# Weight tiles fetched with a shift of three bytes, decoded in three VectorE passes, and the range guard run in the loop on a second read

## The chip, the cores and the metric

The kernel runs on one core of one Trainium2 chip. The metric is the device time of one execution in microseconds (us); 598.0 us is the median of three runs before the change. The engines named below are PE (TensorE, matmuls), PEld (its weight loads), DVE (VectorE), ACT (ScalarE), POOL (GpSimd) and SP (SyncE, which here issues nearly all transfers).

## The reference

An attention-like recurrence over 768 steps (batch 4, 8 heads of 48) feeds a gated feed-forward layer:

```python
for t in range(S):
    cur = np.einsum('bhd,bhe->bhde', u[None] * kt, vt)
    y[:, :, t] = np.einsum('bhd,bhde->bhe', rt, state + cur)
    state = wt[:, :, :, None] * state + np.einsum('bhd,bhe->bhde', kt, vt)
...
gate = 1.0 / (1.0 + np.exp(-(x @ w_gate)))
val = x @ w_val
return (gate * val @ w_out).astype(np.float32)
```

Here x holds the 3072 rows of y with 384 columns; w_gate and w_val are 384 x 1536, w_out is 1536 x 384. The three weight matrices come as 64-bit floats, and the kernel turns them into 32-bit floats itself, by moving bits.

## The kernel before

**Stages.** The 768 steps are cut into 6 chunks of 128; chunk n of batch element b is one attention stage q = 4 n + b, so there are 24 stages. Each stage loads `pin` (decays, k and r, heads on the partitions) and `tok` (r, k and v, time on the partitions), runs two scans on VectorE (prep_k, prep_r), small matmuls on PE (turn_k, scores, sums, mix), a guard on ScalarE (`guard`, a Square with an accumulator) and ends by writing the 384 columns of x for its 128 rows, split into a high part (float32r) and the rest. The feed-forward layer takes 512 rows at a time (n = 0 to 5) and goes through 12 tiles of d_ff (f = 0 to 11). For each f: 9 matmuls into `pg` (gate), 9 into `pu` (value), a sigmoid on ScalarE, the product on VectorE (hidden), its high and low part (hidden_hi on ScalarE, hidden_lo on VectorE), and 9 matmuls into `po` (down). `pg` and `pu` have one buffer each.

**Weights.** A weight tile f is 128 partitions by 1152 words of 64 bits (the gate's, the value's and the output's 384 columns). `fetch` loads it into `raws[f]`, 9216 bytes a partition. `word(f, i)` is the view of its low (i = 0) or high (i = 1) 32-bit words, at a stride of two words. VectorE puts the 32-bit float together in `full` (one buffer): w_body shifts the high word by 3 and masks it (L271), w_sign takes over the top two bits (L275), w_tail the low word's top three (L279). w_hi rounds it to float32r on ScalarE (L284), w_lo takes the rest on VectorE (L287). Both parts are laid over the raw tile. Beside that `w_guard` squares the high words as 32-bit floats on ScalarE and runs a Relu over the squares, each with an accumulator (L265, L266); the two sums per tile tell later whether any weight is outside the range that the decoding takes.

**Head and loop.** The first 13 stages, the decoding of all 12 weight tiles and the feed-forward layer of n = 0 and 1 (in groups of 256 rows, for which `up` and `down` take two stages at a time) stand in an order that a planner (`Plan`) makes when the kernel is built: a list schedule by engine with a cost for each step, ranks for the attention stages and weight tiles (TURNS), a fixed order of transfers (COMES), and counts of free buffers (ROOM). From n = 2 on the order is written out: one step is one f, three steps (i = 0, 1, 2) carry one attention stage of the next chunk. `steps(q)` cuts that stage into `trio[i][0..2]`. In a step every engine takes its part in this order: gate, sigmoid, trio[i][0], value, hidden, hidden_hi, hidden_lo, trio[i][1], the down matmuls of the step before, trio[i][2]. Of this, at i = 0: turn_k and take_k (ScalarE copies kT, L377), then scores_sums, in which `pairs` (L390) is followed by `add_up` (L437), which reads kT. At i = 1: state_mix, take_y, turn_x, take_x, and the loads for stage q + 2. At i = 2: bonus3, bonus4, prep_r of stage q + 1 and, as the last of them, guard of stage q + 1 on ScalarE (L368). Engines run their own instructions in order and wait for each other by semaphores; SP issues its transfers in order.

**The end.** In the first step of n = 5 `check_bounds` compares all accumulators with their limits, adds the results up through a matmul and writes `flag`. If it is set, a general version (`general`) runs after the loop.

Of the kernel before, what the change touches and what calls it, by code (L numbers as in the profile page):

```python
# [9 lines left out]
F32 = mybir.dt.float32  # L10
F32R = mybir.dt.float32r
BF16 = mybir.dt.bfloat16
I32 = mybir.dt.int32
I64 = mybir.dt.int64
AF = mybir.ActivationFunctionType
ALU = mybir.AluOpType
AX = mybir.AxisListType
# [3 lines left out]
DM, DFF = 384, 1536  # L21
P = 128
C = 128
NC_ = S // C
NG = B * NC_
# [3 lines left out]
WW = 520  # L29
NFF = DFF // P  # L30
NKT = DM // P
TINY = 2.0 ** -14
LEAST = float.fromhex("0x1.2p-15")
TURNS = "c0 w0 c1 w1 c2 w2 w3 w4 w5 c3 w6 w7 w8 c4 w9 w10 w11 c5 c6 c7 c8 c9 c10 c11 c12"
COMES = "p0 t0 ub w0 p1 p2 t1 w1 w2 p3 t2 t3 w3 w4 w5 t4 p4 w6 w7 w8 w9 w10 w11 p5 t5 t6 p6 t7 p7 p8 t8 t9 p9 p10 p11 t10 t11 p12 p13 t12 t13"
# [9 lines left out]
def general(ctx: ExitStack, tc: tile.TileContext, dec, tok, wts, u, out, whi, wlo, ident):  # L45
# [72 lines left out]
    def feed(n, b, turned):  # L118
# [6 lines left out]
        for f in range(NFF):  # L125
            for s, acc in enumerate((pg, pu)):
                for k in range(NKT):
                    cols = slice(s * DM + k * P, s * DM + (k + 1) * P)
                    for j, (w, a) in enumerate(((wlo, xhi), (whi, xlo), (whi, xhi))):
                        nc.tensor.matmul(acc[:, :C], lhsT=w[f][:, cols], rhs=a[:, k], start=k == 0 and j == 0, stop=k == NKT - 1 and j == 2)  # L130
            nc.scalar.activation(gate, pg[:, :C], AF.Sigmoid)
            nc.vector.tensor_tensor(out=h, in0=pu[:, :C], in1=gate, op=ALU.mult)
# [72 lines left out]
def tile_kernel(ctx: ExitStack, tc: tile.TileContext, dec: bass.AP, tok: bass.AP, wts: bass.AP, u: bass.AP, out: bass.AP):  # L205
    nc = tc.nc
    const = ctx.enter_context(tc.tile_pool(name="const", bufs=1))
    own = ctx.enter_context(ExitStack())
    own.enter_context(tc.manual_schedule())
    p1 = own.enter_context(tc.tile_pool(name="p1", bufs=1))  # L210
# [25 lines left out]
    for s in range(2):  # L236
        part = after[s * HC:(s + 1) * HC]
        nc.gpsimd.affine_select(
            out=part, in_=part, pattern=[[1, HC]], compare_op=ALU.is_gt, fill=0.0, base=0, channel_multiplier=-1,
# [1 line left out]
    ub = const.tile([P, DM], F32, name="ub")  # L241
    acc_d = const.tile([L, NG], F32, name="acc_d")
    acc_x = const.tile([P, NG], F32, name="acc_x")
    acc_s = const.tile([P, NFF], F32, name="acc_s")
    acc_t = const.tile([P, NFF], F32, name="acc_t")
    fine = const.tile([P, 4, NG], F32, name="fine")
    nc.gpsimd.memset(fine, 1.0)
    flag = const.tile([1, 1], I32, name="flag")
    ones = const.tile([P, 1], F32, name="ones")
# [4 lines left out]
    raws, fulls, whi, wlo = {}, {}, [None] * NFF, [None] * NFF  # L254

    def fetch(f):
        raws[f] = const.tile([P, 3 * DM], I64, tag=f"w{f}", name=f"wraw{f}")
        nc.sync.dma_start(raws[f], wts[f])

    def word(f, i, dtype=I32):  # L260
        return raws[f].bitcast(dtype).rearrange("a (c w) -> a c w", w=2)[:, :, i]

    def w_guard(f):
        sq = p1.tile([P, 3 * DM], BF16, tag="sq", name=f"sq{f}")
        nc.scalar.activation(sq, word(f, 1, F32), AF.Square, accum_out=acc_s[:, f:f + 1])  # L265
        nc.scalar.activation(sq, sq, AF.Relu, bias=1.0, scale=-1.0 / TINY ** 2, accum_out=acc_t[:, f:f + 1])  # L266

    def w_body(f):
        t = p1.tile([P, 3 * DM], I32, tag="full", name=f"full{f}")
        fulls[f] = t  # L270
        nc.vector.tensor_scalar(out=t, in0=word(f, 1), scalar1=3, scalar2=0x3FFFFFF8, op0=ALU.logical_shift_left, op1=ALU.bitwise_and)  # L271

    def w_sign(f):
        t = fulls[f]
        nc.vector.scalar_tensor_tensor(out=t, in0=word(f, 1), scalar=-0x40000000, in1=t, op0=ALU.bitwise_and, op1=ALU.bitwise_or)  # L275

    def w_tail(f):
        t = fulls[f]
        nc.vector.scalar_tensor_tensor(out=t, in0=word(f, 0), scalar=29, in1=t, op0=ALU.logical_shift_right, op1=ALU.bitwise_or)  # L279

    def w_hi(f):
        w = const.tile([P, 2, 3 * DM], F32R, tag=f"w{f}", name=f"w{f}")
# [82 lines left out]
    def guard(q):  # L365
        junk = p1.tile([L, 2, 516], BF16, tag="junk", name=f"junk{q}")
        both = eg[q][:, 1:1 + 2 * 519].rearrange("a (i c) -> a i c", c=519)[:, :, :516]
        nc.scalar.activation(junk, both, AF.Square, accum_out=acc_d[:, q:q + 1])  # L368

# [105 lines left out]
    def parts_x(q):  # L475
        if q // B not in x:
            x[q // B] = p2.tile([P, 2, NKT, B * C], F32R, tag="x", name=f"x{q // B}")
        return (x[q // B][:, j, :, q % B * C:(q % B + 1) * C] for j in range(2))

    def take_x(q):  # L480
        hi, _ = parts_x(q)
        nc.scalar.activation(hi, bank["x", q], AF.Copy, accum_out=acc_x[:, q:q + 1])

# [16 lines left out]
    def gate(n, f, i0, i1):  # L500
        hid["g", n, f, i0] = up(0, "pg", n, f, i0, i1)

    def sigmoid(n, f, i0, i1):
        sg = hid["s", n, f, i0] = stage.tile([P, (i1 - i0) * C], F32, tag="sg", name=f"sg{n}_{i0}_{f}")
        nc.scalar.activation(sg, hid["g", n, f, i0], AF.Sigmoid)  # L505

# [51 lines left out]
    def check_bounds():  # L558
        nc.vector.tensor_scalar(out=fine[:L, 0], in0=acc_d, scalar1=2.0 ** 90, scalar2=None, op0=ALU.is_le)
        nc.vector.tensor_scalar(out=fine[:, 1], in0=acc_x, scalar1=0.0, scalar2=0.0, op0=ALU.mult, op1=ALU.is_equal)  # L560
        nc.vector.tensor_scalar(out=fine[:, 2, :NFF], in0=acc_s, scalar1=1e10, scalar2=None, op0=ALU.is_le)
        nc.vector.tensor_scalar(out=fine[:, 3, :NFF], in0=acc_t, scalar1=0.0, scalar2=None, op0=ALU.is_equal)
        count = p1.tile([P, 1], F32, name="count")
        nc.vector.tensor_reduce(out=count, in_=fine, op=ALU.add, axis=AX.XY)
        total = att_bank("total")
        nc.tensor.matmul(total[:1, :1], lhsT=ones, rhs=count, start=True, stop=True)
        nc.vector.tensor_scalar(out=flag, in0=total[:1, :1], scalar1=float(P * 4 * NG), scalar2=None, op0=ALU.not_equal)


    plan = Plan(ROOM)  # L570
# [3 lines left out]
    def add(name, engine, cost, after, rank, f=None, *args, take=(), give=()):  # L574
        plan.add(name, engine, cost, after, rank, f and (lambda: f(*args)), take, give)

    add("ub", "SP", 0.6, [], comes["ub"], lambda: nc.sync.dma_start(ub, u.partition_broadcast(P)))
    for q in range(3 * B + 2):
        k = rank.get(f"c{q}", 99)
# [33 lines left out]
    for f in range(NFF):  # L613
        k = rank[f"w{f}"]
        add(f"words{f}", "SP", 4.2, [], comes[f"w{f}"], fetch, f)
        add(f"wg{f}", "ACT", 2.8, [f"words{f}", f and f"wg{f - 1}"], k, w_guard, f)
        add(f"wb{f}", "DVE", 0.76, [f"words{f}", f and f"wb{f - 1}"], k, w_body, f, take=["full"])
        add(f"ws{f}", "DVE", 1.36, [f"wb{f}"], k, w_sign, f)
        add(f"wt{f}", "DVE", 1.36, [f"ws{f}"], k, w_tail, f)
        add(f"wh{f}", "ACT", 1.15, [f"wt{f}", f"wg{f}"], k, w_hi, f)  # L620
        add(f"wl{f}", "DVE", 1.3, [f"wh{f}"], k, w_lo, f, give=["full"])
    for g, (n, i0, i1) in enumerate(GROUPS):
        m = i1 - i0
        for f in range(NFF):
            a, name = (n, f, i0, i1), f"{g}_{f}"
            k = 100 + f + LAGS[g]
# [45 lines left out]
    for n in range(2, NC_):  # L672
        for j in range(B):
            trio = steps((n + 1) * B + j) if n + 1 < NC_ else nothing
            for i in range(3):
                a = (n, 3 * j + i, 0, B)
                if a != ahead:
                    gate(*a)
                sigmoid(*a)
                trio[i][0]()  # L680
                value(*a)
                hidden(*a)
                hidden_hi(*a)
                hidden_lo(*a)
                trio[i][1]()
                if last:
                    down_turned(*last.pop())
                trio[i][2]()
                last.append(a)
                if n == NC_ - 1 and j == 0 and i == 0:  # L690
                    check_bounds()
# [37 lines left out]
```

## Time and profile before

| What | us |
|---|---|
| runs shown | 595.76, 598.0, 598.21 |
| median | 598.0 |
| span of the profiled execution, first to last instruction | 593.7 |
| around the span, by the median | 4.3 |
| PE busy, of the span | 555.1 |
| VectorE busy | 332.6 |
| ScalarE busy | 200.2 |

No time is listed for the profiled execution but its span; the runs lie 2.1 to 4.5 us above it. Rows of the profile start with the engine or the line: `L275 DVE ...` is line 275 on VectorE, `out<-in` names the tiles, `x12` counts the instructions, then come busy time and mean length in ns, then the idle time of that engine just ahead of them and who ended it. Rows of a timeline start with two times, start and length.

### The profile page before, as it was taken

To read this page: it belongs to the slowest core of one execution; us is meant where nothing else is said; L and a number is where in the kernel's file an instruction comes from. 1 tells how busy PE (TensorE), PEld (TensorE's weight loads), DVE (VectorE), ACT (ScalarE), POOL (GpSimd) and SP (SyncE) were. 2 spreads that over 40 slices of the span, in tenths; PEclk is the share of its full clock that TensorE was granted. 3 is DMA by queue.
4 is the path that set the end of the run, shared out by engine and by line. 5 is a ranking of instruction groups with operands and counts; after the bars stand their busy time and mean duration, and the time that the engine had idled before them with its cause. 6 is when DMAs were issued, how large, how long until landed. Compare 5 with 4: busy or idle time off the path is not lost.

```text
span 593.7 us, 14287 instructions
## 1 busy us (share of the span) xinstructions
PE 555.1 (93%) x6330; PEld 478.6 (81%) x6330; DVE 332.6 (56%) x571; ACT 200.2 (34%) x397; POOL 96.4 (16%) x86
## 2 busy tenths in 40 slices
PE   4477799999999999999999999999999999999995
PEld 3366699999999999888888888888888888788884
DVE  4989889989675762254644644644544554212121
ACT  2648783434333322322212322212322212222221
POOL 3342011102220503002202202202202200000000
PEclk9998799999999999999999999999999999999999
DMA  8887930022243221122032042032032000100001
GB/s 238 269 332 285 363 94 2 1 88 71 73 135 97 82 70 60 54 87 73 18 88 78 17 135 87 3 87 83 24 124 86 3 1 2 40 15 0 1 0 60
DMA packets 11479, 50.84 MB, mean 86 GB/s; under 512 B 1312, under 2 KB 2464, under 8 KB 9872
## 3 DMA queue, kind: packets, MB, share of 16 engines
q1 hardware_dynamic: 8672, 45.38, 23.7%
q10 hardware_dynamic: 2736, 4.46, 2.0%
q8 instruction: 52, 0.85, 0.6%
q14 instruction: 19, 0.16, 0.1%
HBM read 45.11 MB, written 4.72 MB: 84 GB/s over the span
## 4 chain that ended last, share of the span: by engine, by line
PE 86%; DVE 7%; DMA 3%; issue 1%; ACT 1%; SPq 0%; ACTq 0%; DVEq 0%
PE pu L494 25%; PE pg L494 25%; PE po L546 16%; PE po L529 8%; PE pa L461 3%; PE pa L390 2%; PE pa L400 2%; DMA wraw<-wts 2%; PE pk L373 1%; PE px L473 1%; PE pv L437 1%; DVE eg L341 1%; DMA pin<-dec 1%; PE pa L437 1%; DVE full L275 1%
## 5 line engine op out<-in xcount | busy, mean ns | idle before, releaser
L494 PE MATMUL pu<-x,w 128*128 128x256 f32 (+1 forms) x864 | 171.4, 343 | 0.0
L494 PE MATMUL pg<-x,w 128*128 128x256 f32 (+1 forms) x864 | 169.0, 341 | 1.2 <-DVE w L287 1.2
L494 PEld LDWEIGHTS pg<-x,w 128*128 128x128 f32 x864 | 137.9, 192 | 19.4 <-DVE w L287 1.6
L494 PEld LDWEIGHTS pu<-x,w 128*128 128x128 f32 x864 | 136.7, 192 | 17.1
L512 DVE TENSOR_TENSOR sg<-pu,sg 128x256 f32<-128x256 f32 (+1 forms) x96 | 53.4, 556 | 145.0 <-PE pu L494 144.0
L516 ACT CAST hh<-sg 128x256 fp32r<-128x256 f32 (+1 forms) x96 | 49.1, 512 | 171.2 <-DVE sg L512 170.8
L505 ACT ACTIVATE sg<-pg 128x256 f32<-128x256 f32 (+1 forms) x96 | 46.9, 489 | 139.0 <-PE pg L494 137.7
L546 PE MATMUL po<-hh,w 128*128 128x512 f32 x288 | 89.1, 390 | 0.0
L334 POOL TENSOR_TENSOR bon<-tok,a 128x384 f32<-128x384 f32 x24 | 34.9, 1456 | 277.3 <-DVE a L330 277.3
L520 DVE TENSOR_TENSOR hl<-sg,hh 128x256 fp32r<-128x256 f32 (+1 forms) x96 | 55.2, 575 | 39.1 <-ACT hh L516 39.0
L546 PEld LDWEIGHTS po<-hh,w 128*128 128x128 f32 x288 | 54.1, 188 | 10.8
L546 PE MATMUL po<-hl,w 128*128 128x512 f32 x144 | 58.7, 407 | 0.2 <-DVE hl L520 0.2
L323 POOL TENSOR_TENSOR bon<-tok,ub 128x384 f32<-128x384 f32 x24 | 32.3, 1345 | 114.1 <-DMA tok<-tok 38.4
L529 PE MATMUL po<-w,hh 128*128 128x384 f32 x192 | 49.7, 340 | 0.0
L468 DVE TENSOR_TENSOR bon<-pa,bon 128x192 f32<-128x192 f32 x48 | 15.6, 352 | 48.0 <-PE pa L461 47.9
L529 PE MATMUL po<-w,hl 128*128 128x384 f32 x96 | 34.5, 359 | 6.0 <-DVE hl L520 6.0
L368 ACT ACTIVATE junk<-eg 112x1032 bf16<-112x1032 f32 x24 | 25.6, 1066 | 29.7 <-DVE eg L358 29.6
L529 PEld LDWEIGHTS po<-w,hh 128*128 128x128 f32 x192 | 35.5, 192 | 0.0
L341 DVE TENSOR_TENSOR_SCAN eg<-pin,ends 112x516 f32<-112x516 f32 x24 | 30.0, 1249 | 5.0 <-DMA pin<-dec 5.0
L546 PEld LDWEIGHTS po<-hl,w 128*128 128x128 f32 x144 | 27.0, 188 | 6.2 <-DVE hl L520 0.6
L358 DVE TENSOR_TENSOR_SCAN eg<-pin,heads 112x516 f32<-112x516 f32 x24 | 29.7, 1237 | 0.0
L326 POOL TENSOR_TENSOR bon<-bon,tok 128x384 f32<-128x384 f32 x24 | 27.4, 1140 | 1.7
(68 smaller groups left out, 502.4 us busy)
## 6 DMA issues: line engine op xcount, KB each, us to landing
pin<-dec SPq DMA_DIRECT2D x23, 675.5 KB, 5.3
tok<-tok SPq DMA_DIRECT2D x24, 576.0 KB, 5.8
wraw<-wts SPq DMA_DIRECT2D x12, 1152.0 KB, 12.3
y<-o ACTq DMA_DIRECT2D x11, 256.0 KB, 2.1
y<-o ACTq DMA_DIRECT2D x8, 192.0 KB, 1.9
pin<-dec SPq DMA_DIRECT2D x1, 448.0 KB, 4.0
y<-o SPq DMA_DIRECT2D x1, 256.0 KB, 2.9
pin<-dec SPq DMA_DIRECT2D x1, 227.5 KB, 2.8
```

The source lines that it names most:

```text
L323: nc.gpsimd.tensor_tensor(out=bon[q], in0=tk[q][:, 0:DM], in1=ub, op=ALU.mult)
L326: nc.gpsimd.tensor_tensor(out=bon[q], in0=bon[q], in1=tk[q][:, DM:2 * DM], op=ALU.mult)
L334: nc.gpsimd.tensor_tensor(out=by_head(bon[q]), in0=by_head(tk[q][:, 2 * DM:]), in1=a0, op=ALU.mult)
L341: nc.vector.tensor_tensor_scan(out=e[:, 516:0:-1], data0=t[:, 516:0:-1], data1=ends[:, 516:0:-1], initial=0.0, op0=ALU.mult, op1=ALU.add,)
L358: nc.vector.tensor_tensor_scan(out=e[:, WW:WW + 516], data0=t[:, 0:516], data1=heads[:, 0:516], initial=0.0, op0=ALU.mult, op1=ALU.add,)
L494: nc.tensor.matmul(t, lhsT=w[f][:, cols], rhs=x[n][:, a, k, i0 * C:i1 * C], start=k == 0 and j == 0, stop=k == NKT - 1 and j == 2)
L505: nc.scalar.activation(sg, hid["g", n, f, i0], AF.Sigmoid)
L512: nc.vector.tensor_tensor(out=sg, in0=hid["u", n, f, i0], in1=sg, op=ALU.mult)
L516: nc.scalar.copy(hh, hid["s", n, f, i0])
L520: nc.vector.tensor_tensor(out=hl, in0=hid["s", n, f, i0], in1=hid["hi", n, f, i0].bitcast(F32), op=ALU.subtract)
L529: nc.tensor.matmul(po[n, i][:, :DM], lhsT=h[:, c], rhs=w[f][:, 2 * DM:], start=f == 0 and j == 0, stop=f == NFF - 1 and j == 2,)
L546: nc.tensor.matmul(po[n, k], lhsT=w[f][:, cols], rhs=h, start=f == 0 and j == 0, stop=f == NFF - 1 and j == 2)
```

## The change

The fetch starts 3 bytes into each row, so that byte 3 of a 64-bit word lands at byte 0. The low 32-bit word then holds bits 24 to 55 of the float, and byte 4 holds its top byte. ScalarE's w_top takes that byte, computes 1.125 x + 0.4375, and writes it as an integer over the high word; the lowest five bits of the result are the top five bits of the 32-bit float. VectorE's w_body shifts the low word right by 5, w_join puts the five bits on top. w_sign and w_tail are gone, w_lo stays.

The guard no longer runs over the fetched tiles. In the loop, `see` loads half a weight tile again (576 of 1152 words, unshifted, 576 KB) into the buffer `full`, and one step later `w_guard` runs on it: a Square and two Relus on ScalarE, for values that are too small and too large. 24 halves take the steps from n = 2, f = 0 to n = 4, f = 0. check_bounds compares one more accumulator. The planner's entries change with it.

```diff
     def fetch(f):
         raws[f] = const.tile([P, 3 * DM], I64, tag=f"w{f}", name=f"wraw{f}")
-        nc.sync.dma_start(raws[f], wts[f])
+        nc.sync.dma_start(raws[f].bitcast(U8)[:, :24 * DM - 3], wts[f].bitcast(U8)[:, 3:])
...
-    def w_guard(f):
-        sq = p1.tile([P, 3 * DM], BF16, tag="sq", name=f"sq{f}")
-        nc.scalar.activation(sq, word(f, 1, F32), AF.Square, accum_out=acc_s[:, f:f + 1])
-        nc.scalar.activation(sq, sq, AF.Relu, bias=1.0, scale=-1.0 / TINY ** 2, accum_out=acc_t[:, f:f + 1])
+    def w_top(f):
+        top = raws[f].bitcast(U8).rearrange("a (c w) -> a c w", w=8)[:, :, 4]
+        nc.scalar.activation(word(f, 1), top, AF.Copy, bias=0.4375, scale=1.125)
 
     def w_body(f):
         t = p1.tile([P, 3 * DM], I32, tag="full", name=f"full{f}")
         fulls[f] = t
-        nc.vector.tensor_scalar(out=t, in0=word(f, 1), scalar1=3, scalar2=0x3FFFFFF8, op0=ALU.logical_shift_left, op1=ALU.bitwise_and)
-
-    def w_sign(f):
+        nc.vector.tensor_scalar(out=t, in0=word(f, 0), scalar1=5, scalar2=None, op0=ALU.logical_shift_right)
+
+    def w_join(f):
         t = fulls[f]
-        nc.vector.scalar_tensor_tensor(out=t, in0=word(f, 1), scalar=-0x40000000, in1=t, op0=ALU.bitwise_and, op1=ALU.bitwise_or)
-
-    def w_tail(f):
-        t = fulls[f]
-        nc.vector.scalar_tensor_tensor(out=t, in0=word(f, 0), scalar=29, in1=t, op0=ALU.logical_shift_right, op1=ALU.bitwise_or)
+        nc.vector.scalar_tensor_tensor(out=t, in0=word(f, 1), scalar=27, in1=t, op0=ALU.logical_shift_left, op1=ALU.bitwise_or)
+
+    seen = {}
+
+    def see(g):
+        f, part = divmod(g, PARTS)
+        seen[g] = p1.tile([P, PW], I64, tag="full", name=f"seen{g}")
+        nc.sync.dma_start(seen[g], wts[f][:, part * PW:(part + 1) * PW])
+
+    def w_guard(g):
+        size = seen.pop(g).bitcast(F32).rearrange("a (c w) -> a c w", w=2)[:, :, 1]
+        sq = p1.tile([P, PW], BF16, tag="sq", name=f"sq{g}")
+        few = p1.tile([P, PW], BF16, tag="few", name=f"few{g}")
+        nc.scalar.activation(sq, size, AF.Square, accum_out=acc_s[:, g:g + 1])
+        nc.scalar.activation(few, sq, AF.Relu, bias=1.0, scale=-1.0 / SMALL ** 2, accum_out=acc_t[:, g:g + 1])
+        nc.scalar.activation(few, sq, AF.Relu, bias=-1.0, scale=1.0 / LARGE, accum_out=acc_u[:, g:g + 1])
...
-        nc.vector.tensor_scalar(out=fine[:, 3, :NFF], in0=acc_t, scalar1=0.0, scalar2=None, op0=ALU.is_equal)
+        for i, acc in enumerate((acc_t, acc_u)):
+            nc.vector.tensor_scalar(out=fine[:, 3 + i, :NP_W], in0=acc, scalar1=0.0, scalar2=None, op0=ALU.is_equal)
...
-        add(f"wg{f}", "ACT", 2.8, [f"words{f}", f and f"wg{f - 1}"], k, w_guard, f)
+        add(f"wg{f}", "ACT", 1.15, [f"words{f}"], k, w_top, f)
         add(f"wb{f}", "DVE", 0.76, [f"words{f}", f and f"wb{f - 1}"], k, w_body, f, take=["full"])
-        add(f"ws{f}", "DVE", 1.36, [f"wb{f}"], k, w_sign, f)
-        add(f"wt{f}", "DVE", 1.36, [f"ws{f}"], k, w_tail, f)
-        add(f"wh{f}", "ACT", 1.15, [f"wt{f}", f"wg{f}"], k, w_hi, f)
+        add(f"wt{f}", "DVE", 1.36, [f"wb{f}", f"wg{f}"], k, w_join, f)
+        add(f"wh{f}", "ACT", 1.15, [f"wt{f}"], k, w_hi, f)
...
                 trio[i][1]()
+                guarded = (n - 2) * NFF + 3 * j + i
+                if guarded < NP_W + 1:
+                    if guarded:
+                        w_guard(guarded - 1)
+                    if guarded < NP_W:
+                        see(guarded)
                 if last:
                     down_turned(*last.pop())
                 trio[i][2]()
```

More of the change, by code (lines that the diff above doesn't have):

```diff
@@ L14 @@
 I64 = mybir.dt.int64
+U8 = mybir.dt.uint8
 AF = mybir.ActivationFunctionType
@@ L31 @@
 NKT = DM // P
-TINY = 2.0 ** -14
+SMALL = 2.0 ** -12
+LARGE = 32.0
+PARTS = 2
+NP_W = NFF * PARTS
+PW = 3 * DM // PARTS
 LEAST = float.fromhex("0x1.2p-15")
@@ L243, in tile_kernel @@
     acc_x = const.tile([P, NG], F32, name="acc_x")
-    acc_s = const.tile([P, NFF], F32, name="acc_s")
-    acc_t = const.tile([P, NFF], F32, name="acc_t")
-    fine = const.tile([P, 4, NG], F32, name="fine")
+    acc_s, acc_t, acc_u = (const.tile([P, NP_W], F32, name=n) for n in ("acc_s", "acc_t", "acc_u"))
+    fine = const.tile([P, 5, NG], F32, name="fine")
     nc.gpsimd.memset(fine, 1.0)
@@ L560, in check_bounds @@
         nc.vector.tensor_scalar(out=fine[:, 1], in0=acc_x, scalar1=0.0, scalar2=0.0, op0=ALU.mult, op1=ALU.is_equal)
-        nc.vector.tensor_scalar(out=fine[:, 2, :NFF], in0=acc_s, scalar1=1e10, scalar2=None, op0=ALU.is_le)
-        nc.vector.tensor_scalar(out=fine[:, 3, :NFF], in0=acc_t, scalar1=0.0, scalar2=None, op0=ALU.is_equal)
+        nc.vector.tensor_scalar(out=fine[:, 2, :NP_W], in0=acc_s, scalar1=1e10, scalar2=None, op0=ALU.is_le)
+        for i, acc in enumerate((acc_t, acc_u)):
+            nc.vector.tensor_scalar(out=fine[:, 3 + i, :NP_W], in0=acc, scalar1=0.0, scalar2=None, op0=ALU.is_equal)
         count = p1.tile([P, 1], F32, name="count")
@@ L566, in check_bounds @@
         nc.tensor.matmul(total[:1, :1], lhsT=ones, rhs=count, start=True, stop=True)
-        nc.vector.tensor_scalar(out=flag, in0=total[:1, :1], scalar1=float(P * 4 * NG), scalar2=None, op0=ALU.not_equal)
+        nc.vector.tensor_scalar(out=flag, in0=total[:1, :1], scalar1=float(P * 5 * NG), scalar2=None, op0=ALU.not_equal)
     plan = Plan(ROOM)
```

## The prediction

> **What bounds the kernel now.** I read the page's shares first, then busy time by stage, then the chain of waits in the first 100 us.
>
> ```profile
> span 593.7 us, 14287 instructions
> PE 555.1 (93%) x6330; PEld 478.6 (81%) x6330; DVE 332.6 (56%) x571; ACT 200.2 (34%) x397; POOL 96.4 (16%) x86
> ```
> ```profile
> 0.00:20.00 20.00, 7.13 (x151) 5.71 (x151) 11.00 (x16) 7.43 (x12) 5.36 (x17) 1.00 0.88 238
> 20.00:40.00 20.00, 12.01 (x200) 10.37 (x201) 17.83 (x25) 12.16 (x21) 10.95 (x8) 1.00 0.89 341
> 40.00:60.00 20.00, 15.92 (x260) 14.34 (x259) 18.42 (x28) 14.70 (x26) 4.16 (x4) 0.88 0.72 268
> 60.00:80.00 20.00, 15.90 (x245) 14.33 (x242) 16.81 (x25) 15.85 (x31) 3.86 (x3) 0.87 0.72 261
> 80.00:100.00 20.00, 19.36 (x239) 18.68 (x232) 18.61 (x28) 11.21 (x23) 2.70 (x2) 1.00 0.23 66
> 300.00:400.00 100.00, 100.00 (x1063) 81.41 (x1050) 51.65 (x92) 26.51 (x52) 16.51 (x12) 1.00 0.24 74
> ```
> The columns of a window are its length, then the busy time of PE, PEld, DVE, ACT and POOL, then the granted clock, the DMA share and GB/s. There are two kernels in one span. In the first 80 us PE idles 29 of 80 us (20 minus 7.13, 12.01, 15.92 and 15.90, added up) while VectorE works 18 of each 20. From about 90 us on PE is full: 100.00 of 100 in the loop. So time can be won only in the head, and anything that makes PE wait in the loop is lost whole, however idle ScalarE is there on average (26.51 of 100).
>
> ```profile
> 2.66 11.41 DMA wraw<-wts
> 15.12 1.26 DVE full L275
> 27.30 1.29 DVE full L275
> 41.90 1.27 DVE full L275
> 53.81 1.28 DVE full L275
> 61.30 2.29 PE pg L494 x9
> 70.32 1.32 PE po L529 x6
> ```
> These are pieces of the chain that ended last (start, length, what). The sign pass of L275, which the change deletes, is on it four times. From 70.32 the chain is nearly all PE.
>
> **The change in the head.** It deletes w_sign (L275), the guard's Square and Relu (L265, L266) with their two accumulator reads, and puts one ScalarE Copy per weight tile in their place.
>
> ```profile
> L271 DVE TENSOR_SCALAR full<-wraw 128x1152 int32<-128x1152 int32 x12 | 9.4, 782 | 1.3 <-DMA wraw<-wts 1.3
> L275 DVE SCALAR_TENSOR_TENSOR full<-wraw,full 128x1152 int32<-128x1152 int32 x12 | 16.2, 1350 | 0.0
> L279 DVE SCALAR_TENSOR_TENSOR full<-wraw,full 128x1152 int32<-128x1152 int32 x12 | 17.1, 1426 | 0.0
> ```
> VectorE: 12 x 1.350 = 16.2 us go. The new w_body has one operator where L271 had two; shape and stride are the same, so I take L271's 0.78 us; its ends are 0.78 and 1.35 (L275). w_join has the operands of L279: 1.43, no change. ScalarE's timeline around the second and third tile's guard:
>
> ```profile
> 24.92 1.24 ACT L265 ACTIVATE sq<-wraw 128x1152 bf16<-128x1152 f32 x1
> 26.28 1.16 ACT L266 ACTIVATE sq<-sq 128x1152 bf16<-128x1152 bf16 x1
> 27.62 1.25 ACT L265 ACTIVATE sq<-wraw 128x1152 bf16<-128x1152 f32 x1
> 29.00 1.16 ACT L266 ACTIVATE sq<-sq 128x1152 bf16<-128x1152 bf16 x1
> 30.22 1.15 ACT L284 CAST w<-full 128x1152 fp32r<-128x1152 f32 x1
> ```
> One guard takes 27.62 - 24.92 = 2.70 us of ScalarE, and that goes. w_top reads bytes at a stride of 8 and writes words at that stride. No row has this; the nearest are the cast of L284 (1.15) and the strided Square of L265 (1.25); I take 1.25. So 1.45 us of ScalarE per tile are freed, 17.4 in all.
>
> What of the 16.2 us counts? The chain carries four sign passes ahead of 70.32: 1.26 + 1.29 + 1.27 + 1.28 = 5.1. The fifth tile's is covered: PE's 61.30 group was on the chain then. Later ones run beside a full PE. Off this goes a new wait: w_join needs w_top. For the first tile, landed at 14.07 (2.66 + 11.41), w_top ends about 15.35, and the sign pass of before was due at 15.12: 0.25 us. For later tiles w_top needs only the fetch and can run ahead. If it does not, up to 0.5 us (1.25 minus 0.78) is exposed for each of five tiles, 2.4 in all. **Head: minus 4.9**; ends minus 2.5 and minus 10.6 (rival 2).
>
> The fetch moves 9213 bytes per row from 3 bytes past the row's start, one run as before. I take no cost; no row shows an odd start, so rival 4 prices it. The Trainium skill, page "DMA: Bandwidth & Descriptors", section "How a descriptor splits into AXI transactions", has reads go out from the 256-byte boundary below the start; rows of 9216 bytes would then take 36 transactions either way, and no run here shows it yet.
>
> **The change in the loop.** 24 steps (all of n = 2 and 3, shifted by one) get a half-tile guard on ScalarE: a Square and two Relus of 576 columns, each with an accumulator read. It is issued after trio[i][1], so at i = 2 it stands behind guard(q+1) and ahead of the next step's sigmoid and take_k. Two views of the same step, ScalarE's and PE's timeline (start, length, engine, line, in brackets the idle time before):
>
> ```profile
> 290.65 1.07 ACT L368 ACTIVATE junk<-eg 112x1032 bf16<-112x1032 f32 x1 [2.36 <-DVE eg L358]
> 291.71 0.58 ACT L505 ACTIVATE sg<-pg 128x512 f32<-128x512 f32 x1
> 292.19 0.52 ACT L377 COPY kT<-pk 128x448 f32<-128x448 f32 x1
> 294.23 0.62 ACT L516 CAST hh<-sg 128x512 fp32r<-128x512 f32 x1 [1.52 <-DVE sg L512]
> 298.86 0.60 ACT L505 ACTIVATE sg<-pg 128x512 f32<-128x512 f32 x1 [4.01 <-PE pg L494]
> ```
> ```profile
> 291.07 2.33 PE L494 MATMUL pu<-x,w 128*128 128x512 f32 x9
> 293.33 0.69 PE L390 MATMUL pa<-pin 48*64 48x64 f32 x32
> 293.84 0.62 PE L437 MATMUL pa<-tok,kT 64*64 64x48 f32 x32
> ```
> ScalarE waits for VectorE's scan until 290.65, runs the old guard, then sigmoid and kT with no gap. kT is done at 292.71; PE reads it at 293.84 (L437, add_up). So 1.13 us of room, and the new guard goes in right there.
>
> Its length follows from the old guard's start-to-start times at 1152 columns, above, and one shorter cast:
>
> ```profile
> 41.94 0.41 ACT L516 CAST hh<-sg 128x256 fp32r<-128x256 f32 x1 [2.06 <-DVE sg L512]
> ```
> Square to Relu 1.36, Relu to the next user of its buffer 1.34, Relu to another operation 1.22: together 3.92. Casts took 0.41 at 256 columns and 0.62 at 512, so 0.82 ns a column, 0.47 us for the 576 columns each pass lacks: 3.92 - 1.41 = 2.5 us. The sigmoid then starts at 294.21, kT ends 1.00 later (0.48 and 0.52) at 295.21, and add_up is late by 295.21 - 293.84 = 1.37 us. PE has nothing else in its order to do.
>
> There are 8 such places: i = 2 of four j in n = 2 and four in n = 3, each followed by a step with take_k. **8 x 1.37 = plus 11.0**. Where the passes wait for no buffer, 0.12 (1.34 - 1.22) goes twice: 2.26 us of guard and 9.0 in all; with 0.1 more than my value it is 11.8. At i = 0 and i = 1 the guard fits: after the cast at 294.23, even 1.4 later, ScalarE has until the sigmoid of 298.86, which shifts by the same 1.4.
>
> The rereads go on SP's queue: each waits for the Square before it, and the later pin and tok loads stand behind it.
>
> ```profile
> tok<-tok SPq DMA_DIRECT2D x24, 576.0 KB, 5.8
> ```
> A tok load has the reread's 576 KB and lands 5.8 us after its issue. The tightest reread is issued at about 292.5 and lands by 298.3; its guard then ends near 300.8, under a microsecond after the delayed sigmoid is due and more than a microsecond before VectorE needs it. The loads behind it are for stage q + 2 while q is worked on, so they have all of stage q + 1 to land in, and some microseconds on SP cost nothing; without that cover the guard's wait would be passed on to PE, up to 5.8 at each place. check_bounds gets one more VectorE operation on an already waiting PE: plus 0.2, from this row and the larger sum after it.
>
> ```profile
> L562 DVE TENSOR_SCALAR fine<-acc_t 128x12 f32<-128x12 f32 x1 | 0.2, 164 | 0.0
> ```
> **Sum:** -4.9 + 11.0 + 0.2 = +6.3. On the span that is 600.0. The median of the runs shown, 598.0, lies 4.3 over this span, which I keep as it is: **604.3 us**.
>
> **The rivals.**
> 1. *The loop hides the guard* (faster). For it: ScalarE is 26.51 busy of 100 there. Against: the room ahead of L437 is 1.13 us and the guard fills 2.5. It decides at 1.13: under that, or with guard(q+1) 1.4 us earlier, nothing stalls, and -4.9 + 0.2 gives 593.3.
> 2. *The head gives more* (no change). VectorE ran seven sign passes before PE was full, the first and the last of them:
> ```profile
> 15.04 1.35 DVE L275 SCALAR_TENSOR_TENSOR full<-wraw,full 128x1152 int32<-128x1152 int32 x1
> 83.42 1.35 DVE L275 SCALAR_TENSOR_TENSOR full<-wraw,full 128x1152 int32<-128x1152 int32 x1
> 45.02 0.41 DVE L512 TENSOR_TENSOR sg<-pu,sg 128x256 f32<-128x256 f32 x1
> 46.61 0.39 ACT L516 CAST hh<-sg 128x256 fp32r<-128x256 f32 x1
> ```
> Seven by 1.35 is 9.4; and the cast at 46.61 stood 1.2 behind its input (45.43) because the old guard held ScalarE. If all of it counts, the head gives 10.6, and the sum is +0.6: 598.6. Against it: the chain held only four.
> 3. *The guard's passes pack without gaps* (no change to slightly slower). An accumulating pass of 384 columns is followed 0.48 us later by kT:
> ```profile
> 34.64 0.49 ACT L482 ACTIVATE x<-px 128x384 fp32r<-128x384 f32 x1 [3.27 <-PE px L473]
> 35.12 0.52 ACT L377 COPY kT<-pk 128x448 f32<-128x448 f32 x1
> ```
> With 192 more columns that is 0.64 a pass, 1.9 for three, 0.8 late at 8 places: 6.2, sum +1.5, 599.5. Against it: the second pass reads the first one's output, and 24.92 to 26.28 shows such a pair with a gap. The Trainium skill, page "ScalarE: Activation LUTs", section "What ACT_TABLE_LOAD costs", has 186 ns plus 0.833 ns a column and 93 ns of overlap; an estimate by it is 1.7 us for three passes and a sum near zero, but the trace's Square of 1152 columns was longer (1.24 us against 1.15) and its accumulator read comes on top.
> 4. *The odd start slows the fetch* (slower). The first tile's 1152 KB at the 341 GB/s of the second window are 3.5 us. Twice that puts 3.5 on a chain that starts with this landing, twice if the second tile is late too: 607.8 to 611.3.
>
> **How the numbers follow.** Forecast 0.50, with its own range 600.7 (9.0 in the loop, 6.5 in the head, all five passes) to 607.5 (11.8 and 2.5); rival 1 0.13; rival 2 0.19; rival 3 0.09; rival 4 0.09. The range that leaves out 2 in 10 runs from 596.5, in the lower part of rival 2, to 608.0, at rival 4's near end. A measurement of this kernel can tell about 0.5%, 3.0 us, from no change. Under 595.0 lies rival 1 with a little of rival 2: 0.15. Between 595.0 and 601.0 lie most of rivals 2 and 3 and the forecast's low end: 0.28. Above: 0.57.
>
> **What would show it.** Right: the profile after has PE idle ahead of L437 with ScalarE's kT as releaser, about 1.4 us at 8 places between 265 and 430; in the head the full PE begins some 5 us earlier; the Copy takes 1.15 to 1.25; VectorE's busy time falls by about 16. Wrong: PE without gaps in the loop (rival 1), a head shorter by 9 or more (rival 2), a guard of under 2 us start to end (rival 3), weight fetches that land later (rival 4). The list order in the head is made by a planner whose costs change too; another order of attention and decoding there would move the head's term in a way that no row shows.

## The result, and the profile after

| | before | after |
|---|---|---|
| median of the runs, us | 597.14 (4 runs, 595.76 to 598.21) | 606.26 (4 runs, 605.1 to 606.77) |
| ratio, 95% interval | | 1.0151 [1.0132, 1.0169] |
| profiled execution: span, us | 593.7 | 604.9 |

The changed kernel is slower by 1.5%, 9.1 us by the medians; the forecast was 6.3. Its profiled execution took 606.62 us, 1.7 around its span.

The page of the changed kernel, its shares:

```profile
span 604.9 us, 14413 instructions
PE 554.8 (92%) x6330; PEld 476.6 (79%) x6330; DVE 320.2 (53%) x560; ACT 240.0 (40%) x505; POOL 96.0 (16%) x86
```

PE has the same 6330 matmuls and the same busy time, so all of the loss is idle time of PE. Who ended that idle time tells the view of waits on PE (engine and tile, who released it, us in total, times, longest):

```profile
PE pk L387 <- DVE pin L361: 9.2, 2, 6.0
PE pa L451 <- ACT kT L391: 8.5, 8, 1.1
PE pv L451 <- DVE x L500: 5.6, 2, 5.1
```

The first row stood on the list before too (9.9 us). The second is new: eight waits for ScalarE's kT, the wait that the prediction named (L437 of before is L451 now). The third is one long wait in the head; it was 1.3 us before. The windows of the changed kernel say the same by place (columns as in the prediction):

```profile
20.00:40.00 20.00, 8.73 (x176) 6.94 (x178) 18.79 (x25) 7.76 (x12) 11.19 (x7) 1.00 0.92 345
40.00:60.00 20.00, 18.02 (x261) 16.99 (x256) 16.01 (x23) 12.33 (x20) 5.23 (x4) 1.00 0.44 139
...
300.00:400.00 100.00, 95.76 (x1111) 77.40 (x1110) 46.68 (x83) 52.69 (x121) 16.48 (x12) 1.00 0.46 145
```

The loop's PE is no longer full (95.76 of 100, where it was 100.00), and from 20 to 40 us PE does less than before (8.73 against 12.01).

**The loop.** ScalarE's and PE's timelines of the changed kernel at one of the eight places:

```profile
291.79 1.07 ACT L382 ACTIVATE junk<-eg 112x1032 bf16<-112x1032 f32 x1 [2.36 <-DVE eg L372]
...
292.85 0.70 ACT L291 ACTIVATE sq<-seen 128x576 bf16<-128x576 f32 x1
293.46 0.19 ACT L291 ACTIVATION_READ_ACCUMULATOR sq<-seen 128x1 f32 x1
293.68 0.68 ACT L292 ACTIVATE few<-sq 128x576 bf16<-128x576 bf16 x1
...
294.49 0.68 ACT L293 ACTIVATE few<-sq 128x576 bf16<-128x576 bf16 x1
...
295.17 0.58 ACT L519 ACTIVATE sg<-pg 128x512 f32<-128x512 f32 x1
295.64 0.52 ACT L391 COPY kT<-pk 128x448 f32<-128x448 f32 x1
```
```profile
294.47 0.69 PE L404 MATMUL pa<-pin 48*64 48x64 f32 x32
296.22 0.67 PE L451 MATMUL pa<-tok,kT 64*64 64x48 f32 x32 [1.06 <-ACT kT L391]
```

The guard runs from 292.85 to 295.17, 2.32 us, with the sigmoid and the copy of kT right behind it. PE is done with `pairs` and waits for kT. Before, `add_up` came 0.51 us after the start of `pairs` (293.33 to 293.84); now it comes 1.75 after. One stage of the loop is as long as the distance of two pin loads on SP; the first and the ninth of a row, after and then before:

```profile
254.96 0.33 SPq L315 DMA_DIRECT2D pin<-dec  x1
...
442.56 0.33 SPq L315 DMA_DIRECT2D pin<-dec  x1
```
```profile
255.14 0.33 SPq L301 DMA_DIRECT2D pin<-dec  x1
...
432.29 0.33 SPq L301 DMA_DIRECT2D pin<-dec  x1
```

Eight stages took 187.6 us and had taken 177.2: plus 10.4, or 1.3 each. From that first pin load to the end it is 349.9 against 338.6, plus 11.4.

**The head.** The same two rows show that the changed kernel reaches the loop at 254.96 instead of 255.14: in these two executions the 16.2 us of sign passes that went from VectorE bought 0.2 us. They didn't run at the same clock: from 40 to 80 us the granted clock was 0.88 and 0.87 before, as the prediction's windows show, and is 1.00 in the changed kernel. The long wait in the head, in PE's and VectorE's timelines:

```profile
39.63 1.08 PE L451 MATMUL pv<-tok,kT 64*64 64x48 f32 x28 [5.14 <-DVE x L500]
40.64 2.29 PE L508 MATMUL pg<-x,w 128*128 128x256 f32 x9
```
```profile
34.40 1.43 DVE L274 TENSOR_SCALAR full<-wraw 128x1152 int32<-128x1152 int32 x1
35.75 2.02 DVE L355 TENSOR_TENSOR_SCAN eg<-pin,ends 112x516 f32<-112x516 f32 x1
...
37.90 1.21 DVE L361 TENSOR_TENSOR pin<-pin,eg 112x512 f32<-112x512 f32 x1
39.03 0.54 DVE L500 TENSOR_TENSOR x<-px,x 128x384 fp32r<-128x384 f32 x1
```

PE waits for rest_x (L500). The 28 matmuls that wait are most of those of `sums` (L451): by the program they write two PSUM buffers, one after the other, and the second is the one out of which rest_x still has to read. The first gate group, whose last input is what rest_x writes, stands right behind them in PE's order. VectorE is never idle here, but does other things first: the next tile's w_body and the decays of the fourth stage (prep_k, L355 to L361). The planner, told that a weight tile now costs VectorE 1.36 us less and ScalarE 1.65 less, made another list. In the kernel before, rest_x (L486 there) and the first gate group came sooner:

```profile
35.55 0.54 DVE L486 TENSOR_TENSOR x<-px,x 128x384 fp32r<-128x384 f32 x1
```
```profile
37.16 2.29 PE L494 MATMUL pg<-x,w 128*128 128x256 f32 x9
```

The gate group started at 37.16 and starts at 40.64 now.

### The profile page after: what moved, and what is told of

It reads as the page before. It is cut to its first block, busy times and chain, and to the rows that moved or that the text cites. A ratio compares the mean times of both kernels' runs of the same rounds, so it can differ in the third digit from the quotient of the medians.

```text
span 604.9 us, 14413 instructions
## 1 busy us (share of the span) xinstructions
PE 554.8 (92%) x6330; PEld 476.6 (79%) x6330; DVE 320.2 (53%) x560; ACT 240.0 (40%) x505; POOL 96.0 (16%) x86
## 4 chain that ended last, share of the span: by engine, by line
PE 68%; DVE 14%; ACT 8%; DMA 6%; issue 3%; POOL 0%; ACTq 0%; SPq 0%; DVEq 0%
PE pu L508 20%; PE pg L508 19%; PE po L560 13%; PE po L543 5%; DMA pin<-dec 3%; PE pa L475 3%; DMA tok<-tok 3%; DVE eg L372 2%; PE pa L414 2%; DVE hl L534 2%; DVE sg L526 2%; DVE eg L355 1%; PE pa L404 1%; DVE full L278 1%; ACT hh L530 1%
## 5 line engine op out<-in xcount | busy, mean ns | idle before, releaser
L348 POOL TENSOR_TENSOR bon<-tok,a 128x384 f32<-128x384 f32 x24 | 32.3, 1349 | 307.0 <-DVE a L344 307.0
L355 DVE TENSOR_TENSOR_SCAN eg<-pin,ends 112x516 f32<-112x516 f32 x24 | 30.8, 1282 | 5.9 <-DMA pin<-dec 5.9
L372 DVE TENSOR_TENSOR_SCAN eg<-pin,heads 112x516 f32<-112x516 f32 x24 | 30.5, 1272 | 0.0
```

The source lines that it names most:

```text
L348: nc.gpsimd.tensor_tensor(out=by_head(bon[q]), in0=by_head(tk[q][:, 2 * DM:]), in1=a0, op=ALU.mult)
L355: nc.vector.tensor_tensor_scan(out=e[:, 516:0:-1], data0=t[:, 516:0:-1], data1=ends[:, 516:0:-1], initial=0.0, op0=ALU.mult, op1=ALU.add,)
L372: nc.vector.tensor_tensor_scan(out=e[:, WW:WW + 516], data0=t[:, 0:516], data1=heads[:, 0:516], initial=0.0, op0=ALU.mult, op1=ALU.add,)
```

## The experiments

**1 and 2: is the loop's price the guard's work or its place?** The first version leaves the rereads, the guard on them and its comparisons out (no range guard on the weights). The second keeps them all, and at i = 2 issues the guard ahead of trio[2][1], where ScalarE waits for VectorE's scan; at i = 0 and 1 it stays behind.

```diff
+                if i == 2:
+                    guard_weights()
                 trio[i][1]()
-                guarded = (n - 2) * NFF + 3 * j + i
...
+                if i < 2:
+                    guard_weights()
```

> Leaves the range guard and its rereads out; everything else is the changed kernel. Theory (the loop's price is kT standing behind the guard, 8 places of 1.3 us): the waits of add_up for kT vanish, a stage of the loop lasts 22.1 us again, and the time falls by 10.4 us against the changed kernel, to about 595.9, within 2 us of the kernel before. Rival (part of the loss is in the head): the same waits vanish, but more than 2 us over the kernel before remain.

> At i = 2 the new guard is issued ahead of trio[2][1], in ScalarE's 2.36 us of waiting for the scan, instead of behind guard(q+1). Theory (the place, not the work): the 8 waits for kT fall under 0.1 us each, the time falls by about 10 us against the changed kernel, to about 596, though ScalarE does as much as before. Rival (the load itself: ScalarE's time and 14 MB of rereads): the waits move elsewhere and less than 5 us are won.

Without the guard: 594.47 us, ratio 0.9951 [0.9929, 0.9973]. With the guard ahead: 594.88, 0.9961 [0.9941, 0.9980]. ScalarE at the same place in the second:

```profile
287.11 0.73 ACT L291 ACTIVATE sq<-seen 128x576 bf16<-128x576 f32 x1
...
289.57 1.07 ACT L382 ACTIVATE junk<-eg 112x1032 bf16<-112x1032 f32 x1
...
290.63 0.58 ACT L519 ACTIVATE sg<-pg 128x512 f32<-128x512 f32 x1
291.11 0.52 ACT L391 COPY kT<-pk 128x448 f32<-128x448 f32 x1
```

The three passes run from 287.11 to 289.57, in what had been idle time, and the old guard, sigmoid and kT follow without a gap. From 250 to 450 us the view of PE's waits is empty for both versions. Place alone is worth 606.26 - 594.88 = 11.4 us; work and rereads that are well placed cost 0.4, less than these runs can tell.

**3: how does the loss grow with the guard's length?** As after, but in the steps of i = 2 the third pass is left out (no test for large values on a third of the halves).

```diff
-        nc.scalar.activation(few, sq, AF.Relu, bias=-1.0, scale=1.0 / LARGE, accum_out=acc_u[:, g:g + 1])
+        if g % 3 != 1:
+            nc.scalar.activation(few, sq, AF.Relu, bias=-1.0, scale=1.0 / LARGE, accum_out=acc_u[:, g:g + 1])
```

> The changed kernel without the third guard pass in the 8 steps at i = 2 (those halves are not checked for large values). Theory (kT is late by the guard's length less the room of 1.13 us): a pass is 0.8 us, so each wait of PE for kT falls from 1.06 to about 0.26 us, a stage from 23.44 to 22.65, and the time by 6.4 us, to about 600. Rival (waiting for the reread or the queue behind it sets the price): the waits stay near 1.0 us.

599.91 us, 1.0055 [1.0031, 1.0079]. PE's waits from 250 to 450 us:

```profile
PE pa L453 <- ACT kT L393: 2.0, 8, 0.2
```

One pass and its gap, 0.81 us from start to start (293.68 to 294.49 above), shortened each wait from 1.06 to 0.25 us. 606.26 - 599.91 = 6.4 us, 0.79 at each of 8 places: beyond the room, every microsecond of guard is a microsecond of time.

**4: the planner's new order.** As after, but the planner is told the old costs: 2.8 us for ScalarE's step, and an empty step in place of the sign pass. The list of the head then is that of before, step for step, while the instructions are those of the change. A second version has this and the guard ahead together.

```diff
-        add(f"wg{f}", "ACT", 1.15, [f"words{f}"], k, w_top, f)
+        add(f"wg{f}", "ACT", 2.8, [f"words{f}", f and f"wg{f - 1}"], k, w_top, f)
...
-        add(f"wt{f}", "DVE", 1.36, [f"wb{f}", f"wg{f}"], k, w_join, f)
-        add(f"wh{f}", "ACT", 1.15, [f"wt{f}"], k, w_hi, f)
+        add(f"ws{f}", "DVE", 1.36, [f"wb{f}"], k)
+        add(f"wt{f}", "DVE", 1.36, [f"ws{f}"], k, w_join, f)
+        add(f"wh{f}", "ACT", 1.15, [f"wt{f}", f"wg{f}"], k, w_hi, f)
```

> The planner sees the old costs (2.8 us for w_top, an empty step of 1.36 us in place of the sign pass), which gives exactly the order of the kernel before in the head; the instructions are those of the changed kernel. Theory (the head's gain was eaten by the new order, in which the fourth stage's scan stands ahead of the second stage's rest_x): the first gate group starts near 34 us instead of 40.6, and the time falls by 4 to 5 us against the changed kernel, to about 602. Rival (the sign passes were covered by other waits, whatever the order): the time stays within 1.5 us of the changed kernel.

> The kernel before's order in the head (as in e3) and the guard ahead of trio[2][1] at i = 2 (as in e2), with all the work of the changed kernel. Theory (two separate prices that add up): e3's 601.9 less the loop's 11 gives 591, ratio to the kernel before 0.988 to 0.992. Rival (the two share something, such as PE's idle time ahead of the loop): 594 or more, no better than e2.

Old order: 601.9 us, 1.0065 [1.0036, 1.0094], 4.4 us under the change. Both: 590.86, 0.9905 [0.9873, 0.9937]. In the old order the pin load of the loop's start is issued at

```profile
252.48 0.33 SPq L315 DMA_DIRECT2D pin<-dec  x1
```

2.7 us earlier than before (255.14), although the first weight tile came 2.1 us later in this run: its w_body started at 16.21, and in the kernel before at 14.10. (Its granted clock from 40 to 60 and from 60 to 80 us was 1.00 and 0.91, for 0.88 and 0.87 before, which helps it.) The first gate group started at 36.45 instead of 40.64; 34 was expected. By the medians too the shorter decoding pays where the order is kept, and the new order gives most of it back.

**5: the odd start of the fetch.** As after, but the source starts at the row's first byte (same 9213 bytes), and w_top writes a constant; the decoded weights aren't the reference's.

```diff
-        nc.sync.dma_start(raws[f].bitcast(U8)[:, :24 * DM - 3], wts[f].bitcast(U8)[:, 3:])
+        nc.sync.dma_start(raws[f].bitcast(U8)[:, :24 * DM - 3], wts[f].bitcast(U8)[:, :24 * DM - 3])
...
-        nc.scalar.activation(word(f, 1), top, AF.Copy, bias=0.4375, scale=1.125)
+        nc.scalar.activation(word(f, 1), top, AF.Copy, bias=7.0, scale=0.0)
```

> The fetch starts at the row's first byte, with the same 9213 bytes, and w_top writes a constant: the weights decoded are not the reference's, all instructions, sizes and the order stay. Theory (the odd start costs nothing that counts): the first tile lands within 0.3 us of the changed kernel's 14.6 and the time is the same within 1 us. Rival (the odd start slows the fetch): the first tile lands at 14.1 or sooner, rows of 9213 bytes move faster, and 1 to 3 us are won.

605.62 us, 1.0128 [1.0079, 1.0176], and its interval holds the change's own. The first tile's w_body, which waits for the landing, in this version and in two with the odd start (guard ahead, and old order):

```profile
13.75 0.76 DVE L274 TENSOR_SCALAR full<-wraw 128x1152 int32<-128x1152 int32 x1 [1.04 <-DMA wraw<-wts]
```
```profile
12.20 0.76 DVE L274 TENSOR_SCALAR full<-wraw 128x1152 int32<-128x1152 int32 x1
```
```profile
16.21 0.76 DVE L274 TENSOR_SCALAR full<-wraw 128x1152 int32<-128x1152 int32 x1 [2.54 <-DMA wraw<-wts]
```

The odd starts lie on both sides of the aligned one and 4 us apart. The expectation's narrow band for the landing missed because a landing scatters more than that; an effect of the odd start isn't to be seen under this scatter. The interval of these four runs is some 3 us either way, so a cost below that isn't excluded.

**6: is ScalarE's relief worth something by itself?** The kernel before, with w_guard's two passes and their comparisons left out (no range guard on the weights) and the order kept.

```diff
     def w_guard(f):
-        sq = p1.tile([P, 3 * DM], BF16, tag="sq", name=f"sq{f}")
-        nc.scalar.activation(sq, word(f, 1, F32), AF.Square, accum_out=acc_s[:, f:f + 1])
-        nc.scalar.activation(sq, sq, AF.Relu, bias=1.0, scale=-1.0 / TINY ** 2, accum_out=acc_t[:, f:f + 1])
+        pass
```

> The kernel before with the range guard's two ScalarE passes left out in the head, and nothing else changed, the planner's order included. Theory (ScalarE is covered by VectorE in the head): 33 us of ScalarE work less win under 1.2 us. Rival (the old guard held up hidden_hi and through it PE, as at 46.61): 2 to 3 us are won.

598.54 us, 1.0019 [1.0002, 1.0037]: nothing is won, though 33.5 us of ScalarE are gone (15.0 and 14.0 in the two passes, 2.3 and 2.2 in their accumulator reads). So what the old order gains with the new decoding is put down to VectorE; ScalarE's relief wasn't tried by itself beside the shorter decoding.

**7: which step of the new order costs?** With the guard ahead, one dependency puts rest_x of the second stage in front of prep_k of the fourth, the step that PE was seen waiting behind.

```diff
-        add(f"pk{q}", "DVE", 2.07, [f"pin{q}"], k, prep_k, q, take=["eg"])
+        add(f"pk{q}", "DVE", 2.07, [f"pin{q}", q == 3 and "xl1"], k, prep_k, q, take=["eg"])
```

> e2 with one more condition for the planner: the fourth stage's prep_k starts after the second stage's rest_x. Theory (that one step is what the new order cost): the first gate group starts near 37 instead of 39.4 to 41, PE's wait for rest_x falls from 5.1 to about 2.5 us, and the time falls 2 to 4 us against e2, to about 592. Rival (the order as a whole, not one step): the first gate group starts sooner, but the time stays within 1 us of e2's 594.9.

A miss: 599.34 us, 1.0043 [1.0018, 1.0068], 4.5 us slower than the guard ahead alone. VectorE's timeline, and PE's:

```profile
36.34 2.03 DVE L278 SCALAR_TENSOR_TENSOR full<-wraw,full 128x1152 int32<-128x1152 int32 x1
38.29 0.54 DVE L500 TENSOR_TENSOR x<-px,x 128x384 fp32r<-128x384 f32 x1
...
39.22 1.22 DVE L355 TENSOR_TENSOR_SCAN eg<-pin,ends 112x516 f32<-112x516 f32 x1
```
```profile
38.89 1.09 PE L451 MATMUL pv<-tok,kT 64*64 64x48 f32 x28 [4.53 <-DVE x L500]
39.91 2.29 PE L508 MATMUL pg<-x,w 128*128 128x256 f32 x9
```

The dependency does put rest_x ahead of prep_k, but the planner filled the place with a w_join. PE's wait fell only from 5.1 to 4.5, and the gate group started no sooner (39.91, for 39.37 with the guard ahead alone). So this run doesn't test what it was made for.

Two more versions with the guard ahead give the planner one old cost each: ScalarE's 2.8 us with its chain ("slow top only"), or the empty step of 1.36 ("slow sign only"); and the pair of both was run again.

```diff
-        add(f"wg{f}", "ACT", 1.15, [f"words{f}"], k, w_top, f)
+        add(f"wg{f}", "ACT", 2.8, [f"words{f}", f and f"wg{f - 1}"], k, w_top, f)
```
```diff
-        add(f"wt{f}", "DVE", 1.36, [f"wb{f}", f"wg{f}"], k, w_join, f)
+        add(f"ws{f}", "DVE", 1.36, [f"wb{f}"], k)
+        add(f"wt{f}", "DVE", 1.36, [f"ws{f}", f"wg{f}"], k, w_join, f)
```

> e2 (guard ahead) with the planner told 2.8 us for w_top, but without the empty step of 1.36 us: one half of what separates e2's order from e5's. Theory (the order is what matters, and it follows small changes of the planner's costs): rest_x of the second stage comes ahead of the fourth stage's prep_k, the first gate group starts before 38, and the time lies between e5's 590.9 and e2's 594.9. Rival (only VectorE's promised time matters to the planner): the same as e2 within 1 us.

> e2 with the empty step of 1.36 us on VectorE, but w_top planned at 1.15 us: the other half. Theory: the fourth stage's prep_k moves far behind rest_x, as in e5, and the time is e5's 590.9 within 1.5 us. Rival: it needs both halves, and the time stays near e2's 594.9.

> e5 again, for its interval. Expected 590 to 592, ratio 0.988 to 0.993 to the kernel before.

Slow top only: 599.01 us, 1.0016 [0.9998, 1.0035], outside what was expected of it. It does test the idea of rest_x: PE's wait there is down to 0.9 us and the gate group starts early, and the time is long all the same.

```profile
36.20 2.29 PE L508 MATMUL pg<-x,w 128*128 128x256 f32 x9
```

Slow sign only: 593.41, 0.9931 [0.9907, 0.9956], between its two expectations. Both again: 591.31, **0.9887 [0.9868, 0.9907]**, the version that beats both kernels, by 6.6 us the one before.

**8: does VectorE decode too early?** The traces show the last tile's w_lo at 136.19 before, at 115.13 in the changed kernel and at 131.68 in the fastest version. With the guard ahead, one dependency holds each tile's decoding back until the gate group of the tile before it is done.

```diff
-        add(f"wb{f}", "DVE", 0.76, [f"words{f}", f and f"wb{f - 1}"], k, w_body, f, take=["full"])
+        add(f"wb{f}", "DVE", 0.76, [f"words{f}", f and f"wb{f - 1}", f > 3 and f"pg0_{f - 1}"], k, w_body, f, take=["full"])
```

> As in the version with the guard ahead and the order of the change, but in the planner the decoding of weight tile f (from f = 4) may begin only when the gate matmuls of tile f - 1 have ended, so that no tile is decoded far ahead of its use. In the traces the last tile's decoding ended at 115 us in the changed kernel, at 114 with the guard ahead, at 136 in the kernel before and at 132 in the fastest version so far. Theory (with its new costs the planner crowds the first 100 us of VectorE with decoding that nobody waits for, and attention, which PE needs, is late by it): PE's idle time between 100 and 200 us falls from 3.3 to 1.5 us or less, VectorE is below 80 us busy in the first 100 (84.8), and the time is 592 or less (0.992 of before). Rival (it is not the early decoding, but how the other steps fall between each other): 594.9 as with the guard ahead alone, or more; the planner's own sum for this order is 1.2 us longer than for that one.

596.21 us, 0.9975 [0.9959, 0.9991]: a miss, not faster than the guard ahead alone. Two windows of it, and the same two of the fastest version (both again):

```profile
20.00:40.00 20.00, 8.41 (x184) 6.84 (x184) 18.79 (x24) 7.73 (x13) 11.68 (x8) 1.00 0.89 336
100.00:200.00 100.00, 99.34 (x1511) 94.34 (x1511) 77.48 (x146) 35.04 (x84) 21.21 (x16) 1.00 0.26 81
```
```profile
20.00:40.00 20.00, 14.15 (x257) 12.51 (x256) 15.38 (x25) 9.93 (x16) 10.54 (x8) 1.00 0.95 367
100.00:200.00 100.00, 99.23 (x1488) 94.18 (x1487) 77.12 (x144) 38.63 (x88) 21.03 (x17) 1.00 0.24 74
```

PE's gaps between 100 and 200 us went as the theory said (99.34 busy, where the guard ahead alone has 96.69), but no time came of it: as much was lost in the first 100 us (PE 68.72 busy there against 71.90, both at a granted clock of 1.00). The fastest version has both stretches full, 14.15 of 20 in the early one.

Six lists of the head with the same decoding, all with the guard ahead, PE's busy time in the two stretches (clock 1.00 in both, in all six):

| List | PE, 20 to 40 us | PE, 100 to 200 us | time over before |
|---|---|---|---|
| old costs (both again) | 14.15 | 99.23 | 0.9887 |
| slow sign only | 12.85 | 98.32 | 0.9931 |
| of the change (guard ahead) | 9.00 | 96.69 | 0.9961 |
| paced decoding | 8.41 | 99.34 | 0.9975 |
| slow top only | 12.30 | 96.44 | 1.0016 |
| rest_x first | 9.46 | 96.30 | 1.0043 |

The two fastest are the two that are good in both columns; the other four don't rank by them. The lists span 1.6%, more than the sign passes are worth (some 6.5 us or 1.1%, next section).

The table's two stretches leave out 40 to 80 us, where the clock differs: it was 0.91 to 0.92 for the two fastest and for slow top only, 1.00 for the guard ahead and for paced decoding, and 1.00, then 0.83 with rest_x first. In two lists the runs with a lower mean clock over the execution were the longer ones: with rest_x first 603.43 and 601.54 us at 0.984 and 0.985, 597.14 to 599.61 at 0.992 to 0.994; with the old costs, first time, 594.78 and 594.34 at 0.985 and 0.986, 589.93 to 591.16 at 0.992 to 0.997. So a part of what a median says is clock. It isn't what separates the lists, though. Five of the six have runs at a mean clock of 0.992 to 0.993, and their times don't overlap: old costs 590.01 to 591.73, slow sign only 592.46 to 594.58, paced decoding 595.47 to 597.06, rest_x first 597.14 to 599.61, slow top only 599.89 to 600.34.

Which feature of a list costs stays open: an early rest_x, each of the two costs by itself and early decoding were tried, and none explains the whole. The empty step alone brings back about half of the way from 0.9961 to the pair's 0.9905 and 0.9887. The pair has one thing that neither cost alone has: in its plan w_hi waits for w_top, and w_join doesn't (the edit of experiment 4); that wasn't tried apart.

## Why the prediction was right and where it failed

The time lies in the forecast's own range (600.7 to 607.5), but 606.26 is nearer to rival 4's near end, 607.8, than to the point, 604.3. The number alone decides little; the runs do. By its own steps:

**The loop's term was right.** Forecast 8 x 1.37 = 11.0; the eight stages cost 1.3 each, 10.4 in all, and 11.4 by the runs with the guard moved. The place (ahead of add_up, kT as releaser, eight times) is as named. Its inputs: the guard took 2.32 us for 2.5 forecast, and add_up came 1.24 late (1.75 less 0.51) for 1.37. That leaves a room of 1.08 us (2.32 - 1.24) for 1.13. What PE then waits, 1.06, is not all of the price, since add_up used to start before `pairs` had ended (0.51 after its start, of 0.69); the stage is 1.3 longer. The gap between passes is there, but short: Square to Relu took 0.83 us from start to start (292.85 to 293.68), 0.70 of it the pass itself, and most of the rest the accumulator read of 0.19.

**Rival 1 (the loop hides the guard) fell**, but what spoke for it was right: ScalarE's 26.51 of 100 does leave the time, and with the guard ahead of the wait for the scan nothing stalls. **Rival 3 (passes without gaps) fell**: it gave 1.9 us. The Trainium skill's estimate in that paragraph (page "ScalarE: Activation LUTs", section "What ACT_TABLE_LOAD costs") was 1.7; the trace has 2.32, since an accumulator read of 0.19 stands behind each pass. **Rival 4 (the odd start)** isn't seen: aligned and odd fetches can't be told apart, within the 3 us that the runs can tell.

The rereads cost nothing, as forecast; in the page's groups ScalarE waited for them 2.1 us in all, off PE's path. They land sooner than the bound of 5.8 that was taken from tok (3.6 in the median):

```profile
seen<-wts SPq DMA_DIRECT2D x24, 576.0 KB, 3.6
```

**The head's term failed.** Forecast was -4.9, with ends at -2.5 and -10.6. By the traces it was -0.2; by the medians 9.1 - 11.4 = -2.3, just outside. The profiled execution of before was shorter than its median (593.7 and 1.7 around it, 595.4, against 597.14), which is most of the difference between the two. The step that failed is the one that took four sign passes straight off the chain, as if the rest of the chain stayed as it was. (Its reading that VectorE works 18 of each 20 us in the first 80 holds from 20 us on; in the first window it works 11.00.) The size was near: with the list kept, both together ran 6.4 and 6.6 us under the kernel before, and there the guard costs no time, so the decoding alone brought some 6.5, between forecast and rival 2. What was not priced is the list: the planner's costs are part of the diff, and its new list took 4.4 us back (601.9 against 606.26). The prediction said so as what would make it wrong, but gave it no term and no chance.

The smaller terms, in three rows of the changed kernel's groups:

```profile
L269 ACT ACTIVATE wraw<-wraw 128x1152 int32<-128x1152 uint8 x12 | 15.4, 1285 | 8.0 <-DMA wraw<-wts 8.0
L274 DVE TENSOR_SCALAR full<-wraw 128x1152 int32<-128x1152 int32 x12 | 11.2, 935 | 1.7 <-DMA wraw<-wts 1.6
L278 DVE SCALAR_TENSOR_TENSOR full<-wraw,full 128x1152 int32<-128x1152 int32 x12 | 16.7, 1389 | 0.0
```

w_top is 1.285 for 1.25 forecast, w_join 1.39 for 1.43. w_body was to be 0.78 and is 0.935; in the old list it is 0.782, so the instruction was priced right and the new list puts it beside something that stretches it (last section). That is 1.8 of the 3.8 us by which the fall of VectorE's busy time (12.4) stayed short of the 16.2 forecast; the longer scans are another 1.6 (means of 1282 and 1272 ns against 1249 and 1237, 24 of each). For check_bounds PE waits 1.01 us, for 0.89 before: 0.1 for 0.2 forecast. The relief of ScalarE, which rival 2 counted on, is worth nothing by experiment 6, where the old decoding ran beside it. One rest stays unexplained: behind check_bounds' matmul the changed kernel takes 77.2 us to its end, for 76.4 before and 76.5 with the guard ahead; these 0.8 are most of what the 11.4 up to the end of the span has over the stages' 10.4.

**The frame.** The 4.3 us around the span were taken from a median and a profile of different executions. The runs with both numbers have 1.7. The sum on the span was 600.0 and the span came out at 604.9: nearly all of this difference is the head's 4.7, and 2.6 of it was covered by the offset that was too large. The total is closer than its parts, and that is luck.

## What to carry to other kernels

Work for an engine that is mostly idle is free only at a place where that engine waits: look in its timeline for the instruction that PE needs next, compare the room ahead of it with the length of what is put in, and put it ahead of a wait that is there anyway. Where a diff changes the costs of a planner, the new order is a change by itself: compare a version with the new instructions in the old order, before the costs are touched, look in the trace whether an edit of the plan moved what it was meant to move, and price the new order by running it, since here the list that the planner made from truer costs was the worse one on the chip.

## What was not expected of the hardware

Some VectorE instructions grew where a GpSimd instruction ran. GpSimd's timeline of the changed kernel at the place shown above (34 to 38 us):

```profile
32.95 2.26 POOL L337 TENSOR_TENSOR bon<-tok,ub 128x384 f32<-128x384 f32 x1 [5.91 <-DMA tok<-tok]
35.29 1.39 POOL L340 TENSOR_TENSOR bon<-bon,tok 128x384 f32<-128x384 f32 x1
```

And w_body at a place where GpSimd is idle (it starts nothing until 52.88):

```profile
49.65 0.75 DVE L274 TENSOR_SCALAR full<-wraw 128x1152 int32<-128x1152 int32 x1
```

The w_body of 34.40 took 1.43 us and ended at 35.83, 0.62 after GpSimd's first instruction (35.21). The scan of 35.75 took 2.02, where the mean of before is 1.25, and ended 1.09 after GpSimd's second (36.68). Both ends are those of an instruction that was held until GpSimd was done and then ran at its usual length, but for 0.13 to 0.16 us. The two other long w_body of this kernel (1.46 at 55.92, 1.57 at 84.35) also end 0.62 after a GpSimd instruction (56.76, 85.30). The Trainium skill, page "SBUF — State Buffer", section "SBUF: two separate sides", has such a rule: VectorE and GpSimd share a pair of ports that the one which starts first holds for its whole instruction, while the other is blocked; of VectorE's instructions it counts those in a 2-port mode and those with two inputs in SBUF. The trace agrees for the scan, which has two inputs; w_body has one, and no row here shows in which mode it ran. No run here varied it, so how much of the lists' spread comes from it isn't shown.

The landing of the first weight tile scatters by 4 us from run to run (w_body starts from 12.20 to 16.21 us). Where a head starts with one transfer, this is more than most of its single edits are worth.
